# Retrieval from an attention memory in scaled fp16 halves: one change to a mixed attention and feed-forward kernel

## The chip, the cores and the metric

The kernel runs on one core of a Trainium2 chip. The core has a matrix engine (PE, with its weight loads shown as PEld), a vector engine (DVE), a scalar engine (ACT), a general engine (POOL) and a queue of its own that issues transfers (SP). The metric is the time of one execution in microseconds, as the median of several runs. Lower is better. Engines run in parallel, each works through its own instructions strictly in the order in which the program wrote them, and they wait for each other at semaphores.

## The reference

Two branches read the same x of 2048 rows and 448 features, and a gate mixes them row by row: out = g·A(x) + (1−g)·B(x), with g = sigmoid(x·gate_w). B is a feed-forward layer, silu(x·W1)·W2 with 1792 hidden features. A is attention with 16 heads of 28 features, over 4 segments of 512 rows. Beside ordinary causal attention within the segment, each segment reads a memory that holds all earlier segments:

```
for s in range(N):                       # N = 4 segments
    qs, ks, vs = q[:, :, s], k[:, :, s], v[:, :, s]
    a_dot = softmax(qs @ ks.T * scale + mask) @ vs
    pq = phi(qs)                         # phi(t) = t+1 if t>0 else exp(t)
    num = pq @ M;  den = pq @ z + 1e-6
    a_mem = num / den
    outs.append(g * a_mem + (1 - g) * a_dot)
    pk = phi(ks)
    M = M + pk.T @ vs;  z = z + pk.sum(rows)
o = concat(outs) @ wo
```

The result has to be near fp32 in precision. The first segment reads no memory and the last one writes none, so there are three updates of the memory and three reads of it, each for four groups of four heads: 12 and 12.

## The kernel before

**Numbers in two halves.** Most operands are kept as two fp16 numbers, a high half and the rest (low half). A product is then three passes: high by high, high by low, low by high. Before it is split, a tensor is divided by a power of two near its largest magnitude. `scales` finds that: DVE takes the largest value of each partition, PE transposes this column (line 418), DVE reduces it and keeps its exponent (lines 421 to 425), PE spreads the result to all partitions (line 427), and DVE takes its reciprocal and a copy (lines 431, 432). `halves` then makes the two halves, ACT the high one (line 516), DVE or POOL the low one (line 508, or lines 510 and 511). Every scale that a later step wants (of the queries, the keys, the memory, the feed-forward layer) is a product of two or three of these, made by small DVE instructions with one column each (`vscale`, `qscale`, `kscale`, `others`, `derive`).

**Stages.** The first stage, about 155 us long, projects queries, keys and values, segment by segment and four heads (a group, 112 features) at a time; `proj` and `vproj` are its products, line 540 their matmuls. It ends when the weight buffers are given back. In the second stage causal attention runs on ACT, POOL and DVE with few matmuls (lines 644, 1182, 1216), and the matmuls of the feed-forward layer (line 540 again, and line 1086) fill PE beside them. In the last stage the output projection and the rest of the feed-forward layer run alone.

**The memory**, inside the first stage. From the projected keys in PSUM, ACT makes max(t,0) and exp(t), DVE or POOL joins them to phi(k) (line 829), ACT and DVE make its fp16 halves (lines 843 and 508), and a transposing transfer turns them. `memory` (from line 884) multiplies them with the value halves: for each of 4 row blocks one matmul of 232 columns (line 895: high keys by both halves of the values) and one of 116 (line 897: low keys by high values). DVE adds the two halves of the result (line 906), POOL masks it to its blocks and adds it to the running fp32 sum `macc` (lines 909, 911). ACT and POOL then split the sum into two parts of type fp32r (lines 914, 915), a format in which PE reads 32 bit numbers.

`retrieve` (from line 919) multiplies phi(q), also in two fp32r parts (lines 836 and 838), with these: for each of 4 row blocks one matmul of 232 columns (line 932) and one of 116 (line 933), two blocks to a PSUM bank. DVE adds the halves while it empties each bank (line 938), and POOL and DVE divide by the denominator and write the result to DRAM (lines 941 to 951).

**What sets the order.** A planner in the program (`Sched`) writes out the order of all instructions before anything runs. Each task has an engine, an estimated duration and a priority. The planner keeps a model of the time at which each engine and buffer comes free, gives the next task to the engine that can start one first, and among tasks that can start equally early takes the one of smaller priority. Some tasks may go to DVE or POOL. The constants at the head of the file (VA, VS, KS1, MP, OT1 and others) are priorities or estimated costs.

## Time and profile before

| | us |
|---|---|
| median of 3 runs | 552.25 |
| lowest, highest | 551.41, 553.03 |
| profiled execution, first to last instruction | 551.7 |
| median less that span | 0.55 |
| PE busy | 534.8 (97%) |
| DVE busy | 409.3 (74%) |
| ACT busy | 391.8 (71%) |
| POOL busy | 354.7 (64%) |

The profile names an instruction by its line in the kernel, its engine, and output and inputs by the program's tile names. A busy share of PE of 97% is not PE at its peak: a matmul's record also holds the time in which its result drains, beside the next one's start. So the distance from one matmul's start to the next one's start is the figure to read, and the chain of waits (the work that ended last, followed back from the end) says whether PE or something else sets the end. Times in views by windows and in the timeline are microseconds from the first instruction.

### The profile page before, as it was taken

The page shows a single profiled execution, that of the slowest core. Times are in us where ns is not written, and L with a number is a line of the kernel's source. Part 1 is how long each engine was busy: PE and PEld are TensorE (multiplying, and loading weights), DVE is VectorE, ACT ScalarE, POOL GpSimd, SP SyncE. Part 2 cuts the span into 40 slices and gives each one's busy share as a digit, 9 for nine tenths or more (in the row PEclk, how much of TensorE's full clock was granted, in tenths as well). Part 3 has the DMA queues.
Part 4 walks back from the last instruction along what each step waited for, and adds up shares of the span by engine and source line. Part 5 has one row for each costly group of instructions (what it writes and reads, how often), then busy time and mean ns, then how long its engine had stood idle before and what let it go on. Part 6 is the DMA issues. An engine that isn't in the chain of part 4 may idle for free.

```text
span 551.7 us, 11563 instructions
## 1 busy us (share of the span) xinstructions
PE 534.8 (97%) x4009; PEld 294.7 (53%) x4009; DVE 409.3 (74%) x1074; ACT 391.8 (71%) x688; POOL 354.7 (64%) x519
## 2 busy tenths in 40 slices
PE   4699999999999999999999999999999999999997
PEld 1234655655554556555665555655555555555444
DVE  6889999899789966777666779766987319646473
ACT  1588898986656977899877997878998896402140
POOL 2063254845830689988999987999999995213120
PEclk8689999999999999999999999999999999999999
DMA  8658998885586434312433234434301515698962
GB/s 276 205 175 227 203 236 233 225 226 166 170 233 162 146 100 137 87 42 80 121 102 102 58 98 124 121 103 112 100 18 53 138 49 152 219 241 212 225 160 83
DMA packets 89194, 81.68 MB, mean 148 GB/s; under 512 B 55176, under 2 KB 78856, under 8 KB 89136
## 3 DMA queue, kind: packets, MB, share of 16 engines
q1 hardware_dynamic: 89136, 80.95, 53.1%
q8 instruction: 31, 0.51, 0.4%
q14 instruction: 27, 0.22, 0.1%
HBM read 48.41 MB, written 26.09 MB: 135 GB/s over the span
## 4 chain that ended last, share of the span: by engine, by line
PE 89%; DVE 4%; DMA 4%; ACT 1%; issue 1%; SPq 0%; DVEq 0%; ACTq 0%
PE mm L540 31%; PE mm L1086 23%; PE sc L540 12%; PE sc L1182 6%; PE sc L644 6%; PE cc L1216 6%; DMA rawf<-in_w_dram 2%; PE cc L932 1%; DMA xraw<-in_x_dram 1%; PE cc L895 1%; DVE sizes L388 1%; DVE sc L654 1%; DMA v_scr<-vt 1%; PE sc L640 1%; PE cc L933 0%
## 5 line engine op out<-in xcount | busy, mean ns | idle before, releaser
L1203 POOL TENSOR_TENSOR phl<-pf,phl 128x384 f16<-128x384 f32 (+1 forms) x192 | 189.5, 1008 | 16.2 <-ACT phl L1199 16.2
L1086 PE MATMUL mm<-wb,ghl 128*128 128x448 f16 (+1 forms) x684 | 148.8, 349 | 0.0
L540 PE MATMUL mm<-xh,wa 128*128 128x512 f16 x572 | 141.4, 379 | 0.0
L1187 ACT ACTIVATE pf<-sc,es 128x512 f32<-128x512 f32 (+1 forms) x192 | 109.7, 623 | 19.8 <-PE sc L1182 18.6
L654 DVE CUSTOM_DVE_ANT_0 sc<-sc,mk 128x384 f32<-128x384 f32 (+1 forms) x192 | 104.8, 572 | 20.4 <-PE sc L644 19.1
L1086 PEld LDWEIGHTS <-ghl 128*128 128x128 f16 x684 | 65.0, 97 | 52.5 <-DVE ghl L508 0.3
L1199 ACT ACTIVATE phl<-pf 128x1280 f16<-128x1280 f32 x64 | 81.3, 1277 | 14.9 <-POOL pf L1193 14.9
L540 PEld LDWEIGHTS <-wa 128*128 128x128 f16 x572 | 53.6, 97 | 54.4 <-issue 1.4
L1182 PE MATMUL sc<-ring 86*128 86x512 f16 (+3 forms) x256 | 59.3, 299 | 0.4 <-ACT pf L1187 0.2
L644 PE MATMUL sc<-ring 84*128 84x128 f16 (+3 forms) x256 | 58.2, 299 | 0.1
L1224 DVE TENSOR_REDUCE oraw<-cc 128x116 f32<-128x232 f32 x64 | 25.3, 395 | 30.8 <-PE cc L1216 30.6
L1063 ACT ACTIVATE th<-mm,ths 128x512 f32<-128x512 f32 x52 | 35.8, 699 | 16.0 <-PE mm L540 15.8
L1216 PEld LDWEIGHTS <-phl 128*128 128x128 f16 x1280 | 41.9, 96 | 9.1
L540 PE MATMUL mm<-xh,wqs 128*128 128x512 f16 x176 | 44.5, 390 | 1.0 <-ACT wqs L516 0.7
L551 POOL TENSOR_TENSOR ol<-ol,ml 128x448 f32<-128x448 f32 x12 | 13.7, 1138 | 48.7 <-DMA ol<-o_scr 37.2
L1065 DVE SCALAR_TENSOR_TENSOR mm<-th,mm 128x512 f32<-128x512 f32 x52 | 35.7, 694 | 10.9 <-ACT th L1063 10.9
L1216 PE MATMUL cc<-vg,phl 128*128 128x29 f16 (+1 forms) x1280 | 43.6, 182 | 0.0
L540 PE MATMUL sc<-wvs,xh 128*128 128x450 f16 x176 | 39.9, 368 | 3.1 <-ACT wvs L516 2.1
L540 PE MATMUL mm<-xh,wks 128*128 128x512 f16 x176 | 42.1, 380 | 0.0
L1069 DVE SCALAR_TENSOR_TENSOR ghl<-mm,ghl 128x512 f16<-128x512 f32 x52 | 35.1, 683 | 5.6 <-ACT ghl L1067 5.2
L1182 PEld LDWEIGHTS <-ring 86*128 86x128 f16 x256 | 23.8, 97 | 22.0 <-issue 1.1
L1067 ACT ACTIVATE ghl<-mm 128x512 f16<-128x512 f32 x52 | 30.9, 604 | 6.5 <-DVE mm L1065 6.4
(165 smaller groups left out, 835.9 us busy)
## 6 DMA issues: line engine op xcount, KB each, us to landing
rawf<-in_w_dram SPq DMA_DIRECT2D x26, 256.0 KB
rawf<-in_w_dram SPq DMA_DIRECT2D x28, 224.0 KB
xraw<-in_x_dram SPq DMA_DIRECT2D x16, 256.0 KB
v_scr<-vt SPq DMA_DIRECT2D x16, 232.0 KB
vg<-v_scr SPq DMA_DIRECT2D x16, 232.0 KB
q_scr<-stg SPq DMA_DIRECT2D x16, 224.0 KB
ring<-q_scr SPq DMA_DIRECT2D x16, 224.0 KB
k_scr<-stg SPq DMA_DIRECT2D x16, 224.0 KB
```

The lines of the kernel that those rows point to most:

```text
L540: nc.tensor.matmul(ps(), *p[i], start=(i == 0), stop=(i == n - 1))
L644: nc.tensor.matmul(ps.v[:, u:u + n], rg.v[:KS, 0, hh, i * 128:(i + 1) * 128], rg.v[:KS, 1, hh, :n], start=(i > 0), stop=(i > 0 or j == 3), ...
L654: nc.vector.tensor_tensor_reduce(r, r, MK[:, L - n:], 1.0, NEG, OP.add, OP.max, mx.v[:, hh, i:i + 1])
L1063: e1 = sact(L, lambda ps=ps, th=th: nc.scalar.activation(th.v, ps.v, AF.Tanh, scale=ths[:, s:s + 1]), m, DER[s], takes=[th], uses=[ps], pr ...
L1065: e2 = dve(L, lambda ps=ps, th=th: nc.vector.scalar_tensor_tensor(ps.v, th.v, 1.0, ps.v, op0=OP.add, op1=OP.mult), e1, uses=[ps, th], prio=p0)
L1069: e4 = dve(L, lambda ps=ps, g=g: nc.vector.scalar_tensor_tensor(g.v[:, 1], ps.v, DOWN, g.v[:, 0], op0=OP.mult, op1=OP.subtract), e3, uses= ...
L1086: nc.tensor.matmul(ps.v[:, lo:hi], g.v[:, y, sl], w.v[:, z, lo:hi], start=(j == 0 and i == 0), stop=(j == len(fs) - 1 and i == 2))
L1182: nc.tensor.matmul(ps.v[:, e:e + w], rg.v[:KK, 1, hh, j * 128:(j + 1) * 128], rg.v[:KK, 0, hh, j * 128:], start=True, stop=True)
L1187: ex.append(sact(e, lambda b=b, ps=ps, pf=pf, e=e: nc.scalar.activation(pf.v[:, b, :e], ps.v[:, :e], AF.Exp, scale=es[:, s:s + 1]), m, *ex ...
L1199: hi = copy(1280, lambda hl=hl, flat=flat: nc.scalar.activation(hl.v[:, 0], flat(), AF.Copy), *mk, takes=[hl], uses=[pf], prio=p0 + 2)
L1203: low = pool(w - u, lambda hl=hl, flat=flat, u=u, w=w: nc.gpsimd.tensor_sub(hl.v[:, 1, u:w], flat()[:, u:w], hl.v[:, 0, u:w]), low, uses=[ ...
L1216: nc.tensor.matmul(p[:, i, :2 - z], hl.v[:, z, u:u + 128], vg.v[:, j, hh, :2 - z], start=(z == zs[0] and i == 0), stop=(z == zs[-1] and j ...
```

## The change

It does four things.

1. `retrieve` and `memory` work in scaled fp16 halves throughout. The running sum is divided by a power of two per row, and phi(q) multiplied by it, so that both fit fp16. The row scale comes from the row sums of phi(k), which ACT adds up while it writes the high half (`accum_out`), once all four groups of a segment are there: `rows`, five small DVE instructions per segment. All `memory` tasks of a segment now come behind it in the program's text.
2. In both, the three passes are matmuls of 116 columns that add up in the same PSUM columns, so no half is left to add afterwards. In `memory`, DVE empties PSUM while it multiplies with the mask; POOL adds and multiplies with `nrm`. In `retrieve`, all four blocks share one bank, and ACT empties it with one copy of 464 columns.
3. The scale products are batched: `segment` makes all six of a segment in one instruction, `exponents` those of the attention for all segments, `derive` those of the feed-forward layer for all segments. In `scales`, two instructions do what four did. The segments' scales stand in ascending order, which removes `xi`.
4. The priorities and some estimated costs are redrawn, so that the planner writes another order on all engines.

```diff
-MP = 34.45
-VF = 0.02
-VA = 1.68
-VS = 15.54
+MP = 28.48
...
         def m2():
-            nc.vector.tensor_reduce(few[:, 0:1], ps.v[:n, :128], axis=AX.X, op=OP.max)
-            nc.vector.tensor_scalar(few[:, 1:2], few[:, 0:1], TINY, None, op0=OP.max)
-            nc.vector.tensor_scalar(few[:, 2:3].bitcast(I32), few[:, 1:2].bitcast(I32), 0x7f800000, None,
-                                    op0=OP.bitwise_and)
-            nc.vector.tensor_scalar(diag, identb[:n, :n], few[:, 2:3], 1.0 / UP, op0=OP.mult, op1=OP.mult)
-        t = dve(650, m2, t, *LATER, uses=[ps], prio=prio)
-        t = pe(half(n), lambda: nc.tensor.matmul(ps.v[:, 256:256 + n], oneb[:n], diag, start=True, stop=True),
-               t, uses=[ps], prio=prio)
+            nc.vector.tensor_reduce(few, ps.v[:n, :128], axis=AX.X, op=OP.max)
+            nc.vector.tensor_tensor(diag.bitcast(I32), infd[:n, :n], few.bitcast(I32).to_broadcast([n, n]),
+                                    op=OP.bitwise_and)
+        t = dve(380, m2, t, *LATER, uses=[ps], prio=prio)
...
+    def segment(s, prio, bds, own, nrm, t_own, t_gh):
...
+            v.tensor_scalar(prod[:, s], tw, top[:, s:s + 1], None, op0=OP.mult)
...
+        SEG[s] = QREADY[s] = KREADY[s] = t
...
+    def derive(prio):
...
+        return dve(1100, go, SCALED[W1], SCALED[W2], *SEG.values(), *GDONE, prio=prio)
...
-        mhl = wp.tile([GW, NG, 2, GW + 4], F32R, name="mhl")
+        mhl = wp.tile([GW, NG, 2, GW + 4], F16, name="mhl")
...
-        ring("phq", [GW, 2, L], F32R, 2)
+        ring("phq", [GW, 2, L], F16, 3)
...
+        def rows(s, prio):
+
+            def go():
+                z = [zp[:, i, s] for i in range(5)]
+                r = inv[:GW, s, 0:1]
+                if s:
+                    nc.vector.scalar_tensor_tensor(z[0], zs[:, s], r, zp[:, 0, s - 1], op0=OP.mult, op1=OP.add)
+                else:
+                    nc.vector.tensor_scalar(z[0], zs[:, s], r, None, op0=OP.mult)
+                nc.vector.tensor_scalar(z[1], z[0], TINY, None, op0=OP.max)
+                nc.vector.tensor_scalar(z[2].bitcast(I32), z[1].bitcast(I32), 0x7f800000, None, op0=OP.bitwise_and)
+                nc.vector.reciprocal(z[3], z[2])
+                nc.vector.tensor_scalar(z[4], z[2], sqp[:GW, s + 1:s + 2], None, op0=OP.mult)
+            ROWS[s] = dve(700, go, *ZS[s], PREADY[s], QREADY[s + 1], prio=prio)
...
-                a = copy(L, lambda: nc.scalar.activation(h2.v[:, 0], ph.v, AF.Copy), tp, takes=[h2], uses=[ph],
-                        prio=prio + 2)
-                b = either(L, lambda e: e.tensor_sub(h2.v[:, 1], ph.v, raw(h2.v[:, 0])), a, uses=[ph, h2],
-                        prio=prio + 2)
+                sa = zp[:, 4, s - 1, g:g + 1]
+                a = copy(L + 110, lambda: nc.scalar.activation(h2.v[:, 0], ph.v, AF.Copy, scale=sa), tp, ROWS[s - 1],
+                         takes=[h2], uses=[ph], prio=prio + 2)
+                b = scaled(L, lambda e: rest(e, h2.v[:, 1], ph.v, sa, h2.v[:, 0]), a, uses=[ph, h2], prio=prio + 2)
                 PQ[t] = h2, [a, b]
             else:
                 h2, b = Buf(R["phh"]), Buf(R["phk"])
-                k1 = copy(L + 110, lambda: nc.scalar.activation(h2.v[:, 0], ph.v, AF.Copy, scale=spk[:GW, s:s + 1]), tp,
+                k1 = copy(L + 330, lambda: nc.scalar.activation(h2.v[:, 0], ph.v, AF.Copy, scale=fit3[:GW, s, 1:2],
+                                                                accum_out=zs[:, s, g:g + 1]), tp,
                           KREADY[s], takes=[h2], uses=[ph], prio=prio + 4)
-                k2 = scaled(L, lambda e: rest(e, h2.v[:, 1], ph.v, spk[:GW, s:s + 1], h2.v[:, 0]), k1, uses=[ph, h2],
+                ZS.setdefault(s, []).append(k1)
+                k2 = scaled(L, lambda e: rest(e, h2.v[:, 1], ph.v, fit3[:GW, s, 1:2], h2.v[:, 0]), k1, uses=[ph, h2],
                             prio=prio + 4)
...
             def go():
-                p = ps.v[:GW, :2 * (GW + 4)]
-                q = p.rearrange("p (h t e) -> p h t e", h=4, t=2)
+                p = ps.v[:GW, :GW + 4]
                 for tb in range(TB):
                     vv = vs[tb][0].v[:, 4 * g:4 * g + 4]
-                    nc.tensor.matmul(p, b.v[:, 0, tb], vv.rearrange("p h t e -> p (h t e)"), start=(tb == 0), stop=False,
-                                     skip_group_check=True)
-                    nc.tensor.matmul(q[:, :, 0], b.v[:, 1, tb], vv[:, :, 0], start=False, stop=(tb == TB - 1),
-                                     skip_group_check=True)
-            m = pe((half(232) + half(116)) * TB, go, *done, *[d for v in vs for d in v[1]], takes=[ps],
+                    for i, (y, z) in enumerate(((0, 0), (0, 1), (1, 0))):
+                        nc.tensor.matmul(p, b.v[:, y, tb], vv[:, :, z], start=(tb == 0 and i == 0),
+                                         stop=(tb == TB - 1 and i == 2))
+            m = pe(half(GW + 4) * 3 * TB, go, *done, *[d for v in vs for d in v[1]], takes=[ps],
                    uses=[b] + [v[0] for v in vs], prio=prio)
             ma = macc[:, g].rearrange("p (h e) -> p h e", h=4)
...
             def red():
-                p = ps.v[:GW, :2 * (GW + 4)].rearrange("p (h t e) -> p h e t", h=4, t=2)
-                nc.vector.tensor_reduce(d.v, p, axis=AX.X, op=OP.add)
+                nc.vector.tensor_mul(ma if s == 0 else d.v, ps.v[:GW, :GW + 4].rearrange("p (h e) -> p h e", h=4),
+                                     bds[:, s])
+            r = dve(GW + 84, red, m, PREADY[s], *MH.get((s - 1, g), []), takes=[d], uses=[ps], prio=prio)
 
             def acc():
-                nc.gpsimd.tensor_mul(ma if s == 0 else d.v, d.v, bds[:, s])
                 if s > 0:
                     nc.gpsimd.tensor_add(ma, ma, d.v)
-            r = dve(290, red, m, takes=[d], uses=[ps], prio=prio)
-            r = pool(128 if s == 0 else 320, acc, r, PREADY[s], *MH.get((s - 1, g), []), uses=[d], prio=prio)
-            hi = copy(GW, lambda: nc.scalar.activation(mhl[:, g, 0], macc[:, g], AF.Copy), r, RT.get((s, g)), prio=prio)
-            lo = pool(GW, lambda: nc.gpsimd.tensor_sub(mhl[:, g, 1], macc[:, g], raw(mhl[:, g, 0])), hi, prio=prio)
+                nc.gpsimd.tensor_mul(n.v, ma, nrm[:, s])
+            r = pool(180 if s == 0 else 420, acc, r, takes=[n], uses=[d], prio=prio)
+
+            def fl():
+                return n.v.rearrange("p h e -> p (h e)")
+            k = zp[:, 3, s, g:g + 1]
+            hi = copy(GW + 110, lambda: nc.scalar.activation(mhl[:, g, 0], fl(), AF.Copy, scale=k), r, ROWS[s],
+                      RT.get((s, g)), uses=[n], prio=prio)
...
-            for half in range(2):
-                ps = Buf(BK[RB])
-
-                def go(half=half, ps=ps):
-                    p = ps.v[:, :4 * (GW + 4)].rearrange("p (b z e) -> p b z e", b=2, z=2)
-                    for u in range(2):
-                        sl = slice((2 * half + u) * 128, (2 * half + u + 1) * 128)
-                        nc.tensor.matmul(p[:, u], a.v[:, 0, sl], m, start=True, stop=False)
-                        nc.tensor.matmul(p[:, u, 0], a.v[:, 1, sl], m[:, 0], start=False, stop=True)
-                RT[(s, g)] = pe((ful(232) + ful(116)) * 2, go, *done, *MH[(s - 1, g)], takes=[ps], uses=[a], prio=prio)
-
-                def add(half=half, ps=ps):
-                    p = ps.v[:, :4 * (GW + 4)].rearrange("p (b z e) -> p b e z", b=2, z=2)
-                    nc.vector.tensor_reduce(rr.v[:, 2 * half:2 * half + 2].rearrange("p b h e -> p b (h e)"), p,
-                                            axis=AX.X, op=OP.add)
-                adds.append(dve(530, add, RT[(s, g)], *adds[:1], takes=[] if adds else [rr], uses=[ps, rr], prio=prio))
-            f = pool(40, lambda: nc.gpsimd.tensor_scalar(w.v, rr.v[:, :, :, DH], 1e-6, None, op0=OP.add), *adds,
-                     takes=[w], uses=[rr], prio=prio)
-            f = dve(200, lambda: nc.vector.reciprocal(w.v, w.v), f, uses=[w], prio=prio)
+
+            def p():
+                return ps.v[:, :TB * (GW + 4)].rearrange("p (b h e) -> p b h e", b=TB, h=4)
+
+            def go():
+                for u in range(TB):
+                    o, sl = ps.v[:, u * (GW + 4):(u + 1) * (GW + 4)], slice(u * 128, (u + 1) * 128)
+                    for i, (y, z) in enumerate(((0, 0), (0, 1), (1, 0))):
+                        nc.tensor.matmul(o, a.v[:, y, sl], m[:, z], start=(i == 0), stop=(i == 2))
+            RT[(s, g)] = pe(half(GW + 4) * 3 * TB, go, *done, *MH[(s - 1, g)], takes=[ps], uses=[a], prio=prio)
+
+            e = copy(TB * (GW + 4), lambda: nc.scalar.activation(rr.v, p(), AF.Copy), RT[(s, g)], takes=[rr], uses=[ps], prio=prio)
...
+                    segment(s + 1, o + SS, bds, of, nrm, t_of, t_gh)
...
                 retrieve(t, o + 8)
-            if s < NSEG - 1:
-                memory(t, o + MP)
+            if s < NSEG - 1 and g == NG - 1:
+                rows(s, o + RW)
+                for u in range(t - g, t + 1):
+                    memory(u, 10.0 * u + MP)
```

Three places of the new order. In the rows below, a number ahead of an arrow or at a name's end is a buffer's, and `x3` means three alike in a row.

**DVE, 25 to 33 us into the program.** `vt` is a value projection's low half, `wqs` and `wks` are the low halves of the query and key weights, `sizes` the largest magnitudes of a chunk, `up` and `top` the scales. Before:

```order
L508 SCALAR_TENSOR_TENSOR wqs<-raw_183,up,wqs 128x4x112
L508 SCALAR_TENSOR_TENSOR wqs<-raw_183,up,wqs 128x4x16
L421 TENSOR_REDUCE few_124<-cc 2x1
L422 TENSOR_SCALAR few_124<-few_124 2x1
L423 TENSOR_SCALAR few_124<-few_124 2x1
L425 TENSOR_SCALAR diag_125<-identb,few_124 2x2
L866 SCALAR_TENSOR_TENSOR vt_106<-sc,vt_106 128x16x28
L388 TENSOR_REDUCE sizes<-xraw 128x1 x2
L508 SCALAR_TENSOR_TENSOR wqs<-raw_183,up,wqs 128x4x112 x3
```

With the change:

```order
L913 SCALAR_TENSOR_TENSOR vt_112<-sc,vt_112 128x16x28
L438 RECIPROCAL up<-cc 128x2
L439 COPY top<-cc 128x2
L913 SCALAR_TENSOR_TENSOR vt_113<-sc,vt_113 128x16x28
L422 TENSOR_REDUCE most<-sizes 128x2
L396 TENSOR_REDUCE sizes<-xraw 128x1
L525 SCALAR_TENSOR_TENSOR wqs<-raw_202,up,wqs 128x4x112
L525 SCALAR_TENSOR_TENSOR wqs<-raw_202,up,wqs 128x4x16
```

The second `vt` has moved ahead of the query weights, three more pairs like the last two rows follow without a break, and the three small low halves that POOL made are DVE's. On PE, all 44 matmuls of the first segment's values now stand ahead of the first one of the queries (before: 33 of them), and all 44 of its queries ahead of the first one of its keys (before: 33, and the keys' first ones mixed with values).

**DVE, just ahead of the key weights' low halves.** Before:

```order
L388 TENSOR_REDUCE sizes<-xraw 128x1
L431 RECIPROCAL up<-cc 128x1
L432 COPY top<-cc 128x1
L508 SCALAR_TENSOR_TENSOR wks<-wa,up,wks 128x4x112 x3
L445 TENSOR_SCALAR tg<-top 128x1
```

With the change:

```order
L438 RECIPROCAL up<-cc 128x1
L439 COPY top<-cc 128x1
L925 RECIPROCAL gate<-gate 128x4
L463 TENSOR_SCALAR prod<-tw,top 128x6
L464 TENSOR_SCALAR fit_83<-uw,up 128x2
L467 TENSOR_SCALAR sqp<-fit_83,spm 128x1
L468 TENSOR_SCALAR sqp<-sqp 128x1
L471 TENSOR_TENSOR fit_83<-fit_83,prod 128x1
L472 TENSOR_TENSOR spm<-spm,fit_83 128x1
L476 RECIPROCAL inv<-fit_83 128x2
L852 SCALAR_TENSOR_TENSOR stg<-mm,stg 128x512
L525 SCALAR_TENSOR_TENSOR wks<-wa,up,wks 128x4x112 x4
```

The second segment's scale products, and the low half of a query projection (`stg`), now stand ahead of the key weights, and DVE makes all four chunks of these (before: POOL made the first).

**ACT, where the first stage ends.** `vt` is the last value projection, `gate` the row gate's exponential, `wa` followed by a number a feed-forward weight that goes into a buffer of the second stage, `th` the first use of the feed-forward scales. Before:

```order
L862 ACTIVATE vt_112<-sc 128x16x28
L864 ACTIVATE gate<-sc,tg 128x1
L1063 ACTIVATE th<-mm_2173,ths 128x512
L516 ACTIVATE wa_2200<-rawf,up 128x512
L1067 ACTIVATE ghl<-mm_2173 128x512
L516 ACTIVATE wa_2212<-rawf,up 128x512
```

With the change:

```order
L909 ACTIVATE vt_119<-sc 128x16x28
L911 ACTIVATE gate<-sc,prod 128x1
L985 ACTIVATE amr<-cc 128x464 x2
L533 ACTIVATE wa_2263<-rawf,up 128x512
L533 ACTIVATE wa_2273<-rawf,up 128x512
L1108 ACTIVATE th<-mm_2250,ths 128x512
```

The two weights have moved ahead of the first `th`. That `th` also waits for more: `derive` is one task for all segments now, and waits for the last segment's gates, which come from the `gate` row above.

250 lines of the change are left out of this document (141 added, 109 removed).

## The prediction

> **What bounds the kernel now.** I read the page first, then windows by stage, then PE's timeline where the change touches it, and last the groups of DVE and ACT that it replaces.
>
> ```profile
> span 551.7 us, 11563 instructions
> PE 89%; DVE 4%; DMA 4%; ACT 1%; issue 1%; SPq 0%; DVEq 0%; ACTq 0%
> PE mm L540 31%; PE mm L1086 23%; PE sc L540 12%; PE sc L1182 6%; PE sc L644 6%; PE cc L1216 6%; DMA rawf<-in_w_dram 2%; PE cc L932 1%; DMA xraw<-in_x_dram 1%; PE cc L895 1%; DVE sizes L388 1%; DVE sc L654 1%; DMA v_scr<-vt 1%; PE sc L640 1%; PE cc L933 0%
> ```
>
> The chain that ends last is PE for 89%. Windows by stage say where it is not (PE, PEld, DVE, ACT, POOL busy, then PE's granted clock):
>
> ```profile
> 0.00:18.30 18.30, 7.01 (x20) 2.44 (x21) 12.68 (x40) 6.20 (x10) 4.11 (x26) 0.73 0.83 281
> 18.30:40.00 21.70, 20.24 (x82) 8.45 (x82) 18.35 (x59) 13.38 (x38) 9.62 (x17) 0.83 0.51 171
> 40.00:155.00 115.00, 115.00 (x669) 65.25 (x668) 106.69 (x266) 92.01 (x200) 62.67 (x97) 1.00 0.80 210
> 155.00:182.00 27.00, 26.84 (x133) 12.51 (x132) 23.83 (x56) 18.42 (x32) 2.61 (x7) 1.00 0.75 204
> 182.00:460.00 278.00, 277.71 (x2629) 160.62 (x2629) 194.30 (x565) 236.28 (x370) 257.41 (x355) 1.00 0.33 91
> 460.00:551.70 91.70, 88.02 (x483) 45.39 (x481) 53.46 (x94) 25.50 (x42) 18.25 (x17) 1.00 0.71 194
> ```
>
> From 40 us to the last few us PE is never without a matmul, at full clock, though DVE is at 106.7 of 115 us in the first stage and POOL at 257 of 278 in the second. So matmul time removed after 40 us comes off the end one for one, as long as PE's queue never has to wait; work of other engines counts only where it makes PE wait. Before 40 us it is the other way round: PE waits for the scales.
>
> **The reads of the memory.** The timeline of PE shows one half of a read with other work behind it, and a whole one (start, length):
>
> ```profile
> 140.03 0.46 PE L932 MATMUL cc<-mhl,phq 112*128 112x232 f32 x1
> ...
> 140.62 0.61 PE L540 MATMUL mm<-xh,wqs 128*128 128x512 f16 x2
> ...
> 153.71 0.43 PE L932 MATMUL cc<-mhl,phq 112*128 112x232 f32 x1
> ...
> 154.71 0.55 PE L540 MATMUL sc<-wvs,xh 128*128 128x450 f16 x2
> ```
>
> A half takes 140.62−140.03 = 0.59 us, a whole one 1.00, so a read costs 1.00 to 1.18 us, depending on how it is cut; with 1.09, the twelve cost 13.1. The new read is 12 fp16 matmuls of 116 columns, 1392 columns. Exactly as many are in today's `memory` product (4×232 and 4×116), which is fp16 already:
>
> ```profile
> 144.49 0.26 PE L895 MATMUL cc<-vt,phk 128*112 128x232 f16 x1
> 144.59 0.22 PE L897 MATMUL cc<-vt,phk 128*112 128x116 f16 x1
> 144.64 0.26 PE L895 MATMUL cc<-vt,phk 128*112 128x232 f16 x1
> ...
> 145.10 0.38 PE L540 MATMUL mm<-xh,wqs 128*128 128x512 f16 x1
> ```
>
> That is 0.61 us for 1392 columns, and 0.05 us from the start of a 116-column matmul to the next start. Twelve of these, with a little for four starts more, are 0.63: 7.6 us for twelve reads. **Term 1: −5.5 us** (bounds: 12×1.00−7.7 = −4.3 and 12×1.18−7.3 = −6.9).
>
> `memory` goes from 8 to 12 matmuls at the same columns, from 0.61 to 0.63 us. **Term 2: +0.3** (0 to +0.5).
>
> **What else the change adds there lies under PE.** ACT empties the reads' bank; its nearest row is the value projection's, 448 columns from PSUM. It also reads twelve accumulators:
>
> ```profile
> L862 ACT ACTIVATE vt<-sc 128x448 f16<-128x448 f32 x16 | 8.7, 545 | 9.5 <-PE sc L540 9.5
> L396 ACT ACTIVATION_READ_ACCUMULATOR rawf<-rawf 128x1 f32 x27 | 5.4, 199 | 0.0
> L938 DVE TENSOR_REDUCE amr<-cc 128x232 f32<-128x464 f32 x24 | 15.0, 633 | 3.7 <-PE cc L933 2.0 <-POOL am L947 1.7
> L838 DVE TENSOR_TENSOR phq<-ph,phq 112x512 fp32r<-112x512 f32 x5 | 3.7, 735 | 0.1
> L838 POOL TENSOR_TENSOR phq<-ph,phq 112x512 fp32r<-112x512 f32 x7 | 9.2, 1314 | 0.8 <-ACT phq L836 0.7
> ```
>
> ACT: 12×0.56+12×0.2 = +9.1 us, on 92.0 of 115. DVE: −15.0 (L938 goes), and +5.1 for seven phi(q) low halves that POOL made (7×0.735), so about 97 of 110. POOL loses those 9.2 us and gains two or three small operations per group. I take 0, since what covers it is PE's own queue of projections; uncovered, ACT's part alone would cost 9.1. The new rows of segment products replace about as many small ones and are likewise under PE, except at the start.
>
> **The start.** Here PE waits, and the waits also cost clock:
>
> ```profile
> 26.23 0.55 PE L540 MATMUL sc<-wvs,xh 128*128 128x450 f16 x2
> 27.21 0.27 PE L418 MATMUL cc<-ident,most 128*2 128x128 f32 x1 [0.43 <-DVE most L414]
> 28.21 0.39 PE L540 MATMUL mm<-xh,wqs 128*128 128x512 f16 x1 [0.73 <-ACT wqs L516]
> 28.89 2.21 PE L540 MATMUL mm<-xh,wqs 128*128 128x512 f16 x5 [0.29 <-DVE wqs L508]
> ...
> 33.57 0.59 PE L540 MATMUL mm<-xh,wqs 128*128 128x512 f16 x2
> ```
>
> ```profile
> 25.40:28.80 3.40, 2.04 (x10) 0.57 (x7) 2.78 (x11) 2.86 (x9) 0.00 (x0) 1.00 0.58 189
> 28.80:32.20 3.40, 3.31 (x9) 1.10 (x10) 3.30 (x10) 3.40 (x12) 2.91 (x6) 0.53 0.56 182
> ```
>
> About 1.9 us are lost to waiting for the query weights until 28.89, and half of the next 3.4 us to a clock of 0.53. The Trainium skill ("TensorE: Matmul & The Clock Gate", Part 1) says that a free-running window of 3413 ns decides the clock; the trace agrees, 3.4 us at half clock behind 3.4 us of patchy work. By that rule any new wait of that size would cost 1.7 us beside itself.
>
> The new PE order puts all 44 value matmuls ahead of the queries, 11 more, 11×0.19 = 2.1 us of cover for the query weights; two instructions fewer in each of two scale chains (0.14 each) bring the start forward by about 0.3. If that were all, up to 1.9+1.7 = 3.6 us would come back. But the wait moves on. PE is through with 44 values at about 28.5 and with 44 queries (9.5 us, and about 1.3 of waiting for DVE's four pairs of low halves) at 39.3. Then it wants the key weights:
>
> ```profile
> 39.96 1.86 DVE L508 SCALAR_TENSOR_TENSOR wks<-wa,up,wks 128x448 f16<-128x448 f32 x3
> L807 DVE SCALAR_TENSOR_TENSOR stg<-mm,stg 128x512 f16<-128x512 f32 x32 | 21.6, 679 | 3.1 <-ACT stg L806 1.7 <-ACT pe L824 1.4
> L388 DVE TENSOR_REDUCE sizes<-xraw 128x1 f32<-128x512 f32 x16 | 10.6, 672 | 4.4 <-DMA xraw<-in_x_dram 4.4
> ```
>
> DVE reaches them at 39.96 today. Ahead of them it now has one low half of values more (0.6), one of queries (0.68), three small weight pieces (0.75 in all) and some ten small instructions (1.5), and less: two magnitudes of x (1.3), six steps of the scale chains (0.85) and the earlier start (0.3). That is +1.1: 41.1, so the first key product can go on at 41.7, and PE waits 2.4 us. Its first eleven key matmuls, paced by DVE, end near 44; today PE has done as much work (44 values, 44 queries, 11 keys, 20.2 us at full clock) at 33.57 + 10.8 = 44.4. **Term 3: 0** (−3.6 if DVE is there in time, +2.0 if the wait also halves a window). I take the middle: DVE's queue sets both.
>
> **The end of the first stage.** PE goes over to the feed-forward layer at 155.10. Its tiles of 11 matmuls have four banks, so the fifth, 4×11×0.216 = 9.5 us later, at 164.6, needs the first one emptied.
>
> ```profile
> 157.68 0.69 ACT L1063 ACTIVATE th<-mm,ths 128x512 f32<-128x512 f32 x1 [1.68 <-PE mm L540]
> ...
> 160.29 0.72 ACT L516 ACTIVATE wa<-rawf,up 128x512 f16<-128x512 f32 x1 [0.35 <-DMA v_scr<-vt]
> ```
>
> Now both weights stand ahead of that `th` on ACT, and the second may not start before the last value tile has left (160.29 today, some 0.6 earlier with the new order, where the last read stands behind the last values). `th` then runs at about 160.4, and with the next steps on DVE behind two weight halves the bank is free near 164.3, against 164.6. **Term 4: +0.2** (0 to +1.5). That `derive` now waits for the last gates is covered by the same wait.
>
> Sum: −5.5+0.3+0+0.2 = −5.0. The profiled span of 551.7 becomes 546.7; the median of the runs is 0.55 above that span, so the forecast is 552.25−5.0 = **547.2 us**. The second and third stages keep their instructions; they only start earlier.
>
> **Rivals.**
>
> *The start gives more* (chance 0.17). If DVE gets to the key weights two or three us sooner than by my count, terms 1 to 4 come to −8: 544. For it: DVE is idle for 3.3 of the 21.7 us from 18.3. Against: the order of DVE, 15 instructions between the second segment's scale and the key weights, where there were two.
>
> *New waits eat the gain* (0.19). PE's order is fixed and longer chains feed it; ACT has 9 us more. A wait of 2 us with a half-clock window at the start, and 1 or 2 us at the end of the first stage, leave 551. For it: term 4's margin of 0.3 us. Against: no wait of PE at all over 115 us today with DVE at 93%.
>
> *Slower by the barrier* (0.06). Reads of a segment now wait for `rows`, which waits for all four groups of the segment before it. From the last phi(k): ACT about 0.9, five small DVE steps about 1, ACT 0.7 and DVE 0.75, 3.4 us, and whatever stands ahead in their queues. If each of the three segments' first reads came to the head of PE's queue too early by 3 us, PE would lose 9 us: 547.2+9 = 556. It decides from 2.3 us each. Against it: PE's order leaves some 77 matmuls, about 16 us, between the last keys of the first segment and the first read.
>
> *Slower by weight loads* (0.02). There are 96 loads more as instructions of their own. If each short matmul paid for its load, at the 96 ns of an average one in this row,
>
> ```profile
> L1216 PEld LDWEIGHTS <-phl 128*128 128x128 f16 x1280 | 41.9, 96 | 9.1
> ```
>
> 288 of them are 27.6 us in place of 13.1+7.3: 559. It decides from 71 ns each. Against: today's 116-column fp16 matmuls start 50 ns apart with loads of their own. The Trainium skill (the same page, "Back-to-back issue gap") gives about 81 ns for a sustained stream of loads and matmuls at 128 columns; by that the two products together would cost 23.3 us, 2.9 more than today, and this trace speaks against it.
>
> **How the numbers follow.** The forecast itself (545.4 to 549) has 0.56. A difference under 0.3%, 550.6 to 553.9, is what a measurement of this kernel can't tell from none. Faster than that: the forecast, the richer start and a third of the eaten gain, 0.79. Within it: the rest of the eaten gain, 0.13. Slower: the last two, 0.08. The range leaves out the slower rivals, the worst of the eaten gain and the best of the start: 543.5 to 552.5.
>
> **What would show it.** The reads as 144 matmuls 50 ns apart, with about 0.63 us from the first to what follows; PE's first wait moved from the query to the key weights, near 40 us, and the first stage over near 150; no line of `retrieve` or `memory` as a wait of PE. I am wrong if those matmuls start 70 ns or more apart, if PE has waits within the first stage, or if the time from 18 to 45 us changes by more than 3 us.

## The result, and the profile after

The changed kernel takes 548.82 us (median of 4 runs, 548.41 to 549.07) against 552.64 us beside it (4 runs, 551.41 to 553.38): a ratio of 0.9926, with a 95% interval of 0.9909 to 0.9944, or 3.1 to 5.0 us less. A second comparison gave 0.9914 (0.9893 to 0.9935). 547.2 was forecast, in a range of 543.5 to 552.5. The time is right; most of the terms behind it are not.

The page after, its span and chain:

```profile
span 546.7 us, 11714 instructions
...
PE 83%; ACT 5%; DVE 5%; DMA 4%; issue 2%; POOL 1%; SPq 0%; DVEq 0%; ACTq 0%
```

The span is 5.0 us shorter than the 551.7 of before, the forecast's own figure, while the medians differ by 3.8. A run's time is 1.7 us above its span (548.41 and 546.7 here; 552.85 and 551.1 in another execution of the kernel before). So the execution of before that was profiled took about 553.4 (an estimate from that distance), the top of its runs, and not 552.25 as the forecast's "0.55 above that span" has it.

Windows by stage of the changed kernel (columns as before: PE, PEld, DVE, ACT, POOL busy, then PE's clock, the DMA engines' busy share and GB/s):

```profile
15.30:40.00 24.70, 22.53 (x101) 9.80 (x101) 22.74 (x71) 18.15 (x46) 3.79 (x11) 0.89 0.69 221
40.00:151.30 111.30, 109.61 (x747) 59.46 (x746) 94.32 (x215) 96.74 (x218) 55.78 (x97) 1.00 0.81 206
151.30:178.00 26.70, 26.70 (x137) 12.71 (x135) 21.96 (x54) 19.25 (x31) 8.95 (x13) 1.00 0.67 188
```

and the same start in the kernel before, cut at its first value product:

```profile
16.80:40.00 23.20, 20.77 (x83) 8.55 (x83) 19.82 (x62) 14.88 (x40) 9.62 (x17) 0.81 0.53 177
```

Two things are to be seen. At 40 us PE has begun 101 matmuls where it had begun 83: 18 more, of about 0.2 us each, or 3.6 us, though the forecast put the start at 0. And between 40 us and the end of the first stage PE is no longer without a gap: 109.6 of 111.3 us. What PE waited for, longest first (total, times, longest):

```profile
PE cc L426 <- DVE most L422: 2.8, 2, 1.7
PE cc L433 <- DVE diag L430: 2.2, 3, 1.2
PE sc L557 <- ACT wvs L533: 2.1, 1, 2.1
PE cc L982 <- DVE phq L525: 1.2, 1, 1.2
...
PE mm L557 <- DVE wks L525: 1.1, 1, 1.1
```

The rows for the query weights (`wqs`) are gone. New, of 1 us and more, are one wait in a read (L982), for a low half of phi(q), and one for the low half of the key weights.

The new operations cost what was forecast from their nearest rows (busy time, mean ns of one):

```profile
L982 PEld LDWEIGHTS <-phq 112*128 112x128 f16 x144 | 8.4, 97 | 4.1 <-DVE phq L525 1.7 <-ACT phq L882 0.3
L525 DVE SCALAR_TENSOR_TENSOR phq<-ph,zp,phq 112x512 f16<-112x512 f32 x12 | 9.2, 768 | 0.8 <-ACT phq L882 0.7
L985 ACT ACTIVATE amr<-cc 128x464 f32<-128x464 f32 x12 | 6.8, 564 | 4.1 <-POOL am L992 2.1 <-PE cc L982 1.8
L888 ACT ACTIVATION_READ_ACCUMULATOR phh<-ph,fit 112x1 f32 x12 | 2.4, 203 | 0.0
```

The eviction on ACT is 0.564 us (0.56 forecast), an accumulator 0.203 (0.2), a low half 0.768 (0.735).

### The profile page after: what moved, and what is told of

The parts are those of the page before. It is cut to its first block, busy times and chain, and to the rows that moved or that the text cites. A ratio compares the mean times of both kernels' runs of the same rounds, so it can differ in the third digit from the quotient of the medians.

```text
span 546.7 us, 11714 instructions
## 1 busy us (share of the span) xinstructions
PE 530.8 (97%) x4105; PEld 290.4 (53%) x4105; DVE 400.3 (73%) x1031; ACT 400.3 (73%) x712; POOL 340.4 (62%) x517
## 4 chain that ended last, share of the span: by engine, by line
PE 83%; ACT 5%; DVE 5%; DMA 4%; issue 2%; POOL 1%; SPq 0%; DVEq 0%; ACTq 0%
PE mm L557 30%; PE mm L1131 23%; PE sc L557 10%; PE sc L1227 6%; PE sc L661 6%; PE cc L1261 6%; DMA rawf<-in_w_dram 2%; DVE xh L525 1%; DMA xraw<-in_x_dram 1%; DVE sizes L396 1%; PE cc L942 1%; PE cc L982 1%; ACT rawf L404 1%; PE sc L657 1%; DMA h_scr<-stg 1%
## 5 line engine op out<-in xcount | busy, mean ns | idle before, releaser
L1244 ACT ACTIVATE phl<-pf 128x1280 f16<-128x1280 f32 x64 | 81.2, 1271 | 13.8 <-POOL pf L1238 13.7
L1227 PE MATMUL sc<-ring 86*128 86x512 f16 (+3 forms) x256 | 58.6, 299 | 0.3 <-ACT pf L1232 0.3
L661 PE MATMUL sc<-ring 84*128 84x128 f16 (+3 forms) x256 | 56.7, 299 | 0.0
L557 PE MATMUL mm<-xh,wqs 128*128 128x512 f16 x176 | 41.7, 379 | 0.0
L1227 PEld LDWEIGHTS <-ring 86*128 86x128 f16 x256 | 24.2, 97 | 22.0
L557 PE MATMUL sc<-wos,oT 128*128 128x448 f16 x176 | 35.4, 352 | 0.0
```

Source lines behind the costliest of these rows:

```text
L557: nc.tensor.matmul(ps(), *p[i], start=(i == 0), stop=(i == n - 1))
L661: nc.tensor.matmul(ps.v[:, u:u + n], rg.v[:KS, 0, hh, i * 128:(i + 1) * 128], rg.v[:KS, 1, hh, :n], start=(i > 0), stop=(i > 0 or j == 3), ...
L1227: nc.tensor.matmul(ps.v[:, e:e + w], rg.v[:KK, 1, hh, j * 128:(j + 1) * 128], rg.v[:KK, 0, hh, j * 128:], start=True, stop=True)
L1244: hi = copy(1280, lambda hl=hl, flat=flat: nc.scalar.activation(hl.v[:, 0], flat(), AF.Copy), *mk, takes=[hl], uses=[pf], prio=p0 + 2)
```

## The experiments

### What a read costs: operands changed, and reads doubled

The forecast's largest term, −5.5 us, rests on 1.09 us for a read in fp32r. In the timeline of PE before, one half of a read with what stands around it reads so when the window is cut finer:

```profile
139.56 0.82 PE L540 MATMUL mm<-xh,wqs 128*128 128x512 f16 x3
140.03 0.46 PE L932 MATMUL cc<-mhl,phq 112*128 112x232 f32 x1
140.33 0.22 PE L933 MATMUL cc<-mhl,phq 112*128 112x116 f32 x1
...
140.62 0.39 PE L540 MATMUL mm<-xh,wqs 128*128 128x512 f16 x1
```

Three matmuls of 512 columns need 3 × 0.216 = 0.65 us, so the next one has its turn at 140.21. Yet the fp32r one is recorded at 140.03, which is 0.03 us after the start of the third, and its record is 0.46 long where those of its kind are 0.33. Its record begins 0.19 us too early, and the forecast counted that stretch as part of the read. There are 18 such places (0.16 us each behind matmuls of 450 columns): 3.3 of the 13.2 us.

`b_f16` and `b_f16b` (the same kernel twice: the profiled execution of the first took 3084 us, so only the second's trace is read) change only the operands' type, with the order and the matmuls of before:

```diff
-        mhl = wp.tile([GW, NG, 2, GW + 4], F32R, name="mhl")
+        mhl = wp.tile([GW, NG, 2, GW + 4], F16, name="mhl")
...
-        ring("phq", [GW, 2, L], F32R, 2)
+        ring("phq", [GW, 2, L], F16, 2)
```

> The kernel before, with the two parts of phi(q) and of the memory's sum as fp16 in place of fp32r; the row scales are left out, so small parts lose precision. Matmuls and the order of all engines are the same. Theory 1 (the prediction's): a read takes 1.09 us, and 0.61 with fp16 operands at the same columns, so the twelve give 12 x 0.48 = 5.8 us, 546.5. Theory 2: the record of an fp32r matmul behind an fp16 one starts 0.028 us after that one's start, though the fp16 one itself takes 0.216; 18 such places hold 18 x 0.187 = 3.4 us that belong to the projections. Then a read takes 0.82, and the change gives 2.4 us, 549.9. No effect on the start under either.

> The kernel before with fp16 operands in its reads (row scales left out) once more, for a usable profile: the first look timed 1.2 us less than before, with an interval of 0.3 to 2.0. Theory 2: the reads' matmuls are 0.100 and 0.053 us apart, 7.3 us in all in place of 13.2, and the 18 matmuls ahead of them have their 0.19 to 0.22 us back in place of 0.028, so that the first stage is 2.4 us shorter. Theory 1: those matmuls stay at 0.028, and the first stage is 5.8 us shorter. If less than 2.4 arrives at the end, a wait after the first stage has taken it.

Measured: 551.35 against 552.36 us, ratio 0.9978 (0.9963 to 0.9994), and 550.30 against 552.16, ratio 0.9966 (0.9947 to 0.9984). That is 1 to 2 us, far from the 5.8 of theory 1. The same place in PE's timeline:

```profile
138.41 0.81 PE L540 MATMUL mm<-xh,wqs 128*128 128x512 f16 x3
139.06 0.26 PE L932 MATMUL cc<-mhl,phq 112*128 112x232 f16 x1
...
139.36 0.60 PE L540 MATMUL mm<-xh,wqs 128*128 128x512 f16 x2
```

The three matmuls ahead have their 0.65 us back. Taken from their start to the start of the one behind the half, it was 1.06 and is 0.95: a half costs 0.41 in fp32r and 0.30 in fp16, a read 0.82 and 0.61, and twelve give 2.5 us. From the first value product to the feed-forward layer, the first stage takes 137.0 us in `b_f16b` and 138.3 before: 1.3 less. Three small waits of 0.32 to 0.35 us, which before has not, took about 1.0 of the 2.5. So theory 2 holds, and even its size does not arrive in full.

`b_dbl` and `a_dbl` price a read with nothing beside it to confuse the records, by issuing all its matmuls twice:

```diff
-                    for u in range(2):
+                    for u in (0, 1, 0, 1):
```

> The kernel before, with every matmul of the reads issued twice, the second time over the same result. Theory 1: the reads cost their 13.1 us once more, 565.4. Theory 2: a half costs 2 x (0.166 + 0.060) = 0.45 us more, 24 of them 10.8 us, 563.1; less than 10 would say that even this is not paid.

> The changed kernel, with every matmul of the reads issued twice. If a 116-column fp16 matmul costs 0.050 us, as in the memory's product, +7.2 us, 556.0. If each paid for its weight load of 0.096 us, +13.8 us, 562.6.

Measured: `b_dbl` 562.11 us, ratio 1.0174 (1.0150 to 1.0198), 9.6 us more (8.3 to 10.9), 0.80 us for a read. Theory 1's 13.1 lies outside; theory 2's 10.8 just within. The trace is closer: from the first value product to the feed-forward layer `b_dbl` takes 149.05 us where before takes 138.25, 10.8 more, or 0.90 for a read. `a_dbl` 555.19 us, ratio 1.0046 (1.0032 to 1.0061); less the 0.9926 of the changed kernel that is 6.6 us more, of 7.2 expected at 0.050 us a matmul and 13.8 if each had paid for its weight load. Its groups:

```profile
L982 PE MATMUL cc<-mhl,phq 112*128 112x116 f16 x288 | 17.0, 214 | 0.6 <-DVE phq L525 0.6
L982 PEld LDWEIGHTS <-phq 112*128 112x128 f16 x288 | 15.9, 97 | 3.1 <-DVE phq L525 0.8
```

A doubled read and what follows it, in PE's timeline:

```profile
151.09 1.40 PE L982 MATMUL cc<-mhl,phq 112*128 112x116 f16 x24
152.33 1.24 PE L557 MATMUL mm<-xh,wks 128*128 128x512 f16 x5
```

24 matmuls in 1.24 us are 52 ns each, so the added ones cost 12 × 0.62 = 7.4 us. Against the changed kernel, waits within two reads fell by 0.9 us (from 1.39 to 0.78 in the last one, from 0.29 to none in the third), which leaves 6.5. Weight loads of 97 ns stay hidden under matmuls 50 ns apart: their records overlap, 288 of them are busy for 15.9 us.

### Where the start's 3.6 us come from: order, or shorter chains

`a_oldc` is the changed kernel with the 21 constants of before, `b_newc` the kernel before with the 21 new ones; two of them:

```diff
-VA = -23.59
+VA = 1.68
...
-OT1 = -81.6
+OT1 = -16.51
```

> The changed kernel with the priorities and estimated costs of the kernel before (21 constants; the new one, of the rows, stays). Theory A: the gain at the start comes from the redrawn order (the second value ahead of the query weights), so that the wait for the query weights and the half clock behind it come back, about 3.6 us, and the wait of 1.25 us for the key weights goes: 551. Theory B: it comes from the shorter chains of the scales alone, and the order does nothing: 548.8 within 1 us.

Measured: 555.64 us, ratio 1.0056 (1.0043 to 1.0069), slower than both kernels, and than both theories say. Up to the end of the first stage theory A holds. PE waits at the query weights' scales again and pays with half a clock behind it, the key weights' wait is gone, and the first stage ends at 153.64 in place of 151.34, 2.3 us later where A has 3.6 − 1.25 = 2.35. PE at that place, and the two clock windows there:

```profile
26.17 0.27 PE L426 MATMUL cc<-ident,most 128*2 128x128 f32 x1 [0.43 <-DVE most L422]
27.67 0.16 PE L433 MATMUL cc<-diag,oneb 2*128 2x2 bf16 x1 [1.22 <-DVE diag L430]
```

```profile
25.20:28.62 3.42, 1.76 (x10) 0.76 (x10) 3.29 (x10) 2.92 (x9) 1.25 (x4) 1.00 0.73 205
28.62:32.03 3.41, 3.41 (x11) 1.28 (x10) 3.41 (x14) 3.41 (x12) 1.74 (x5) 0.50 0.64 198
```

The rest is lost behind it, where neither theory looked: from there to the last matmul PE takes 396.1 us in place of 391.5, with single waits in the second and last stage, of which this one is the longest,

```profile
469.01 1.24 PE L557 MATMUL mm<-xh,wa 128*128 128x512 f16 x5 [1.53 <-DVE ghl L1114]
```

so old constants do not fit the new task list.

> The kernel before with the priorities and estimated costs of the changed kernel (21 constants), nothing else changed. Theory A: the redrawn order carries the start's gain by itself, with no wait for the query weights, and the end comes 2 us sooner, 550.5. Theory B: the constants fit only their own program, as those of before did, which in the changed kernel cost 4.6 us after the first stage: slower than 552.5 whatever the start does.

Measured: 566.88 us, ratio 1.0259 (1.0239 to 1.0280), 14.3 us slower: theory B. Its start does gain, with no wait at the query or key weights. The matmuls that PE begins from the first value product to 40 us tell the order from the chains; here in `b_newc` (new order, old chains) and in `a_oldc` (old order, short chains):

```profile
16.70:40.00 23.30, 22.24 (x99) 9.82 (x99) 21.49 (x71) 16.83 (x44) 8.46 (x15) 0.88 0.62 198
15.10:40.00 24.90, 22.22 (x88) 9.44 (x88) 22.46 (x63) 17.31 (x47) 5.07 (x13) 0.80 0.55 182
```

These are 99 and 88, beside 83 before (85 in its second profile) and 101 in the changed kernel. So the order alone brings 16 of the 18 matmuls, the shorter chains alone 5; together they add little to the order, because PE then reaches the key weights ahead of DVE and waits.

But from 116 us on it waits in the middle of reads, for scale chains and for the low half of phi(q) that POOL makes there, and half a clock follows the longest of these. Its first stage ends 8.2 us later than before, and 4.1 more are lost behind it. Two of its waits, and the clock windows around them:

```profile
PE cc L427 <- DVE diag L425: 5.8, 4, 1.9
...
PE cc L933 <- POOL phq L838: 2.1, 1, 2.1
```

```profile
118.07:121.49 3.42, 0.76 (x5) 0.61 (x5) 3.35 (x13) 2.98 (x7) 0.93 (x3) 1.00 0.91 216
121.49:124.90 3.41, 2.81 (x15) 2.29 (x14) 3.12 (x20) 2.38 (x5) 1.26 (x1) 0.50 0.69 227
...
159.03:162.45 3.42, 1.17 (x8) 0.59 (x5) 1.06 (x3) 2.35 (x5) 2.71 (x5) 1.00 0.40 113
162.45:165.86 3.41, 3.41 (x13) 1.74 (x13) 2.16 (x8) 0.00 (x0) 0.87 (x4) 0.50 0.29 100
```

Neither half of the change is a gain alone at its full size: the operands give 1 to 2 us, the order on the old program costs 14, the program in the old order costs 3, and both together gain 4.

`a_m4` puts back the chain's four small DVE instructions:

```diff
...
-            nc.vector.tensor_tensor(diag.bitcast(I32), infd[:n, :n], few.bitcast(I32).to_broadcast([n, n]),
-                                    op=OP.bitwise_and)
+            nc.vector.tensor_scalar(few[:, 1:2], few[:, 0:1], TINY, None, op0=OP.max)
+            nc.vector.tensor_scalar(few[:, 2:3].bitcast(I32), few[:, 1:2].bitcast(I32), 0x7f800000, None,
+                                    op0=OP.bitwise_and)
+            nc.vector.tensor_scalar(diag, identb[:n, :n], few[:, 2:3], None, op0=OP.mult)
```

> The changed kernel with the four small DVE instructions per scale chain that the kernel before has, in place of two; order and the rest unchanged. Theory 1: a chain is 0.40 us longer (0.85 against 0.45 from its first to its last DVE instruction), two chains in series stand ahead of the first value product, and PE starts 0.8 us later, near 16.0; the end comes 0.8 to 1.6 us later, 548.8 to 549.5 beside the 547.9 of the changed kernel in the last comparison. Theory 2: the earlier start was scatter between executions (it was 14.7 to 15.9 in five of them), and nothing changes.

Measured: 549.59 us, ratio 0.9951 (0.9937 to 0.9965), 1.4 to 2.0 us above the two readings of the changed kernel. The first chain on PE, here and in the changed kernel:

```profile
10.03 0.27 PE L426 MATMUL cc<-ident,most 128*1 128x128 f32 x1 [4.14 <-DVE most L422]
11.94 0.16 PE L435 MATMUL cc<-diag,oneb 1*128 1x1 bf16 x1 [1.64 <-DVE diag L433]
```

```profile
9.04 0.27 PE L426 MATMUL cc<-ident,most 128*1 128x128 f32 x1 [1.66 <-DVE most L422]
10.55 0.16 PE L433 MATMUL cc<-diag,oneb 1*128 1x1 bf16 x1 [1.24 <-DVE diag L430]
```

The first chain has 1.91 us from PE to PE where it has 1.51: 0.40 more, and 0.83 for the two ahead of the first value product. Theory 1 holds in its size per chain. The rest of the later start in this execution (17.12 in place of 14.7 to 16.1 in six executions of the changed order) stands ahead of the chain, at the first matmul's 10.03 (7.9 to 9.8 in those six), so it is not the chain's; I take it for scatter.

### The two new waits of PE

Both wait for DVE, each behind something that could go later. `a_keys` and `a_tail` move rows on DVE and nothing on PE; `a_both` does both. (With the first move, one copy on ACT also falls behind another.) In rows of DVE's order:

```diff
 RECIPROCAL gate<-gate 128x4
+SCALAR_TENSOR_TENSOR wks<-wa,up,wks 128x4x112 x4
+SCALAR_TENSOR_TENSOR stg<-mm,stg 128x512
 TENSOR_SCALAR prod<-tw,top 128x6
...
-SCALAR_TENSOR_TENSOR stg<-mm,stg 128x512
-SCALAR_TENSOR_TENSOR wks<-wa,up,wks 128x4x112 x4
```

```diff
-SCALAR_TENSOR_TENSOR wa<-rawf,up,wa 128x512
 SCALAR_TENSOR_TENSOR phq<-ph,zp,phq 112x512
+SCALAR_TENSOR_TENSOR wa<-rawf,up,wa 128x512
```

> The changed kernel with one change on DVE: the four low halves of the key weights, and the low half of the third query product behind them, come ahead of the second segment's scale products. PE's order is the same. Theory 1: DVE's queue sets PE's wait of 1.25 us at the first key product. The key weights' first low half then starts at 36.0 in place of 38.0, ahead of PE at 37.35, the wait goes, and with it 1.25 us: 547.5. Theory 2: the wait moves on, to a bank that is emptied later or to the products that need the late scales: no gain, 548.8.

> The changed kernel with one change on DVE: the low half of the last phi(q) comes ahead of a feed-forward weight's low half of about 0.75 us. PE's order is the same. Theory 1: the wait of 1.39 us in the last read is DVE's queue as to 0.75 us, and the rest is ACT's high half: 548.1, with the first stage over 0.75 us sooner. Theory 2: the weight's low half is then late, or the first stage ends with something else (the last value's transfer), and nothing comes off: 548.8.

> The changed kernel with both moves, of the key weights and of the last phi(q). If both theories 1 hold, 1.25 + 0.75 = 2.0 us: 546.8. If the end of the first stage is set by something that doesn't hang on the start, the gain of the key weights alone is lost and returns here.

> The changed kernel as it is, beside the three above: 548.8. Waits of 1.25 us at the first key product and 1.39 us in the last read again, if they come from the order; other places or sizes, if they were chance.

Measured in one comparison, as ratios to before: `a_same` 547.88 us, 0.9914 (0.9893 to 0.9935); `a_keys` 547.52, 0.9896 (0.9878 to 0.9915); `a_tail` 547.99, 0.9912 (0.9894 to 0.9929); `a_both` 547.00, 0.9898 (0.9878 to 0.9918). The four overlap, so no gain over the changed kernel is shown by times. The traces say more. In `a_same` the waits come back at the same places (1.35 us at the first key product, 1.40 in the last read), so the order makes them. The last read in the changed kernel, and with the move in `a_tail`:

```profile
149.32 0.27 PE L982 MATMUL cc<-mhl,phq 112*128 112x116 f16 x2
150.81 0.69 PE L982 MATMUL cc<-mhl,phq 112*128 112x116 f16 x10 [1.23 <-DVE phq L525]
151.34 1.03 PE L557 MATMUL mm<-xh,wa 128*128 128x512 f16 x4
```

```profile
148.33 0.27 PE L1000 MATMUL cc<-mhl,phq 112*128 112x116 f16 x2
149.17 0.69 PE L1000 MATMUL cc<-mhl,phq 112*128 112x116 f16 x10 [0.57 <-DVE phq L541]
...
152.43 0.81 PE L573 MATMUL mm<-xh,wa 128*128 128x512 f16 x3 [0.19 <-ACT amr L1003]
```

The start distance from the second to the third matmul of that read goes from 1.44 to 0.78 us, as theory 1 of `a_tail` has it. But a new wait follows 3 us later, for ACT to empty the read's bank, and from the first feed-forward matmul to the last PE takes 391.8 us where `a_same` takes 391.0: the gain is given back, as theory 2 has it for the end. Of these 0.8 us 0.36 are that wait, and the rest two smaller ones (0.19 and 0.27) near 455 and 460 us. In `a_keys` the key products start without the wait of 1.25 us, but two of 0.3 stay at their next chunks, the first of them behind POOL, which makes the small low halves of the key weights:

```profile
36.94 1.67 PE L573 MATMUL mm<-xh,wks 128*128 128x512 f16 x7
38.78 2.43 PE L573 MATMUL mm<-xh,wks 128*128 128x512 f16 x9 [0.17 <-POOL wks L544]
```

Theory 1 of `a_keys` holds for half of the wait there; in `a_both` the key products run without any wait. `a_both` ends its first stage at 149.05 where `a_same` does at 150.66, though its start was 0.9 us later, and gives 0.9 back behind it. Its span of 544.8 us is the shortest of all; its time is not separated from that of the changed kernel.

### The scatter of the kernel before

> The kernel before as it is, for a second profile. Its times lie within 551.0 and 554.4, while the changed kernel's lie within 1 to 2 us. Theory 1: the half-clock window behind the wait for the query weights comes and goes with where the clock's windows fall, which is worth up to 1.7 us; the first profile held it in full, so that the profiles differ by 5.0 us and the medians by 4. Then this one shows another size or place of that window. Theory 2: the window is always there, and the scatter comes from elsewhere.

Measured: 552.75 us, ratio 1.0001 (0.9988 to 1.0014). Its profile has the waits for the query weights of the first one within 0.01 us and half a clock behind them again, so that this window comes and goes is not shown. But the clock does take part in the scatter, which theory 2 denies. Every timed run has its mean granted clock on record. Of the 51 runs of the kernel before that stood beside the experiments, the 7 at 0.991 took 550.6 to 551.6 us, and the 11 at 0.984 or 0.985 took 552.8 to 554.4. A mean lower by 0.0065 is 0.0065 × 551 × 2 = 7 us more at half clock, an estimate, or about two windows of 3.4 us. The two profiles have 0.984 and 0.987, so no trace shows which windows the quickest runs go without. Nor is the clock all of it: from 0.986 to 0.988 the times go from 551.4 to 554.2. Part may be the first value product (16.47 here, 16.85 in the first profile, 14.68 to 16.05 in six executions of the changed order).

## Why the prediction was right, and where it was not

**Term 1, the reads, −5.5: mis-sized, and the reading failed.** The step that failed is "A half takes 140.62−140.03 = 0.59 us": start to start, from an fp32r matmul that is recorded while the fp16 one ahead is still streaming. A read cost 0.82 us, not 1.09. In the changed kernel it is 0.62, as forecast (twelve in about 7.5 us, waits aside), so the gain is 2.4, less 1.7 for two waits within reads (1.39 in the last, 0.29 in the third). The bound of −4.3 came from the same reading and fell with it.

**Term 2, `memory`, +0.3:** from 7.33 to 7.78 us, +0.45.

**Term 3, the start, 0: mis-sized by all of its lower bound.** It gave −3.6. The mechanism was right: the wait for the query weights and the half clock went, and the wait moved to the key weights. Its size was not. DVE began the key weights' low halves at 38.00, not at 41.1: 2.0 us sooner than before, where the forecast had 1.1 later. PE lost 1.25 us where 2.4 were reckoned.

```profile
35.62 1.90 PE L557 MATMUL mm<-xh,wqs 128*128 128x512 f16 x8
37.35 0.38 PE L557 MATMUL mm<-xh,wks 128*128 128x512 f16 x1
38.82 0.38 PE L557 MATMUL mm<-xh,wks 128*128 128x512 f16 x1 [1.09 <-DVE wks L525]
```

Three sizes in that count were wrong. The start came 1.5 us sooner (first value product at 15.33 for 16.85), where "two instructions fewer in each of two scale chains (0.14 each) bring the start forward by about 0.3". The chains bring 0.83 of it, since each small instruction holds up the chain for 0.18 us, its record of 0.14 and what lies between two, and the last one is shorter too; the rest was not told from scatter. From the first value product to the key weights DVE was idle for 3.4 us before and for 2.0 now (19.73 us busy of 23.11, and 20.71 of 22.67), where the count left the idle time as it was. And DVE's work there grew by 1.0 us, where the items of the count come to 1.4. The order alone, with the old chains, brings DVE to the key weights at 38.36 (`b_newc`), so the chains are not the main part.

This is the rival "The start gives more" in its mechanism and nearly in its size, and DVE's idle time, which was the argument for it, is part of what gave way. It came together with a term 1 that gave 2.4 us in place of 5.5, and 0.7 after its waits. That the sum still fell near the forecast is luck: two errors of over 3 us had opposite signs.

**The wait that nobody forecast** is the 1.4 us in the last read. The forecast put "+9.1 us, on 92.0 of 115" on ACT and said "I take 0". Elsewhere ACT and DVE were covered but for three waits of about 0.3 us, but at the stage's end PE has no more projections to cover with, and a feed-forward weight's low half stood ahead of phi(q)'s on DVE:

```profile
148.97 1.12 DVE L525 SCALAR_TENSOR_TENSOR wa<-rawf,up,wa 128x512 f16<-128x512 f32 x1
150.02 0.74 DVE L525 SCALAR_TENSOR_TENSOR phq<-ph,zp,phq 112x512 f16<-112x512 f32 x1
```

"PE has waits within the first stage" was named as a sign of being wrong, and it is there.

**Term 4, +0.2:** no wait of PE shows in the stretch from 151.34 to 178 (26.70 of 26.70 us busy), so 0. The first `th` began at 155.48, 4.1 us behind the start of the feed-forward layer, early enough for its bank.

**The ledger.** The first stage ends at 151.34 in place of 155.10: −3.8. Of it −3.6 at the start, −2.4 in the reads, +1.7 for waits in reads, +0.45 in `memory`, and +0.7 for two waits of 0.3 us, at 84.7 and 124.0 us; these come to −3.15, and 0.6 stay unassigned. From there to the last matmul PE takes 391.5 us where it took 392.7. These 1.2 us were not forecast. They lie in the score products (L640, L644 and L1182, now L657, L661 and L1227), whose start distances sum to 71.6 in place of 72.8 us. Of it 0.9 is L1182's, 36.2 us before and 35.3 after (36.2 and 35.2 in the second profiles), which had small waits of 0.1 to 0.4 us; why there are fewer was not tested.

**The rivals.** "New waits eat the gain": they came, 3.6 us in five places (1.25, 1.39, and three of about 0.3), without a half-clock window behind them, and the start paid for them. "Slower by the barrier": no read waits for `rows` in the trace. "Slower by weight loads": `a_dbl` puts an added matmul at 0.046 to 0.051 us, not 0.071 or more. The Trainium skill ("TensorE: Matmul & The Clock Gate", "Back-to-back issue gap") gives some 81 ns for each matmul of a sustained stream with loads at 128 columns; the 24 pairs of a 116-column matmul and its load in a row, 52 ns each in `a_dbl`, do not bear it out.

## What to carry to other kernels

Don't price a group of matmuls from its first recorded start when the one ahead is of another type: take the distance between two matmuls of the same kind around the group, less what those need alone. A term that lies "under" the bound engine is covered only as long as that engine has queued work left, so the last piece of each stage is to be followed by itself. Where a planner sets the order, the task list and its constants are one thing: either alone lost 3 to 14 us here, both together gained 4.

## What the runs showed of the hardware that was not expected

**Records of fp32r matmuls behind fp16 ones** start about 0.03 us after the start of the fp16 one, whose columns need 0.19 to 0.22 us. In fp16, at the same place, they start when those are over.

**Weight loads in fp32r** take 191 ns for 112x128 and 97 ns in fp16 (before, and `b_f16b`):

```profile
L932 PEld LDWEIGHTS cc<-mhl,phq 112*128 112x128 f32 x48 | 9.2, 191 | 2.4 <-POOL mhl L915 0.4
```

```profile
L932 PEld LDWEIGHTS <-phq 112*128 112x128 f16 x48 | 4.6, 97 | 2.2
```

Within a whole read of before, the fp32r loads start 0.11 us apart (64.62, 64.74, 64.85, 64.96 us), two of them 0.22, and a pair of its matmuls, of 232 and of 116 columns, takes 0.166 + 0.060 = 0.226 us; in fp16 the pair takes 0.100 + 0.050. So the loads' pace would explain why a read costs more in fp32r, and why each doubled one cost 0.90; no run separates it from the matmuls themselves.

**The clock was not halved by waits of 1.25 and 1.4 us** in the changed kernel, against the prediction's "any new wait of that size would cost 1.7 us beside itself":

```profile
37.63:41.05 3.42, 2.33 (x12) 1.06 (x12) 3.42 (x7) 3.42 (x8) 0.35 (x2) 1.00 0.86 246
41.05:44.46 3.41, 3.41 (x18) 1.59 (x17) 3.35 (x6) 3.00 (x7) 0.00 (x0) 1.00 0.67 198
```

PE was busy for 68% of that window, and the next ran at full clock; so did those behind the two windows around the last read (80% and 84%). In the windows shown, 51% busy (`a_oldc`, 25.20), 22% and 34% (`b_newc`, 118.07 and 159.03) were each followed by half a clock, as was one of 57% before (25.62). The Trainium skill ("TensorE: Matmul & The Clock Gate", Part 1) has the gate look at free-running windows of 3413 ns, which these edges bear out, and return to half rate after an idle window; here windows that were half busy, with no single gap over 1.5 us, did so too. What share decides can't be told: one of 58% in `a_oldc`, at 465.52, was followed by full clock, and in `b_newc` the half clock of 121.49 went on for another window though PE was busy for 82% of it.
